# First and last pair of a spectral mixer kernel: other orders of the channel transforms, and the last token transform in other banks

## The chip, the cores and the metric

The kernel runs on one core of one Trainium2 chip. The metric is the device time of one execution in microseconds (us), as the median of several runs of the same kernel. Less than 0.2% (0.73 us) between two kernels is what such a comparison can hardly tell from no change.

## The reference, cut to what matters

The input `x` is 2048 tokens by 512 channels. It is normalised over the channels; then two branches are computed from the same normalised `xn`, multiplied, and added to `x`:

```
xn = layernorm(x)
s  = irfft2(rfft2(xn) * (w_r + 1j * w_i))        # over tokens and channels
g  = silu((gelu(xn.T @ w1 + b1) @ w2 + b2).T)    # a two-layer MLP over the tokens, width 1792
out = x + s * g
```

So a row of the output needs its piece of the inverse spectral transform (`s`) and its piece of the second MLP product (`g`).

## The kernel before, in words

The first 200 us of the program (layer norm, forward transforms, the first MLP product, the spectral filter) are not touched. What is touched is the last stage, the loop over `p` in 0..7. Tokens are held as 16 output tiles of 128 tokens by 512 channels; pair `p` makes tiles `p` and `p + 8` (the names `j0` and `j1`).

**MLP part of a pair.** The second MLP product of a pair is done with a seven-product scheme (as in Strassen's): `ORDER = (1, 2, 5, 6, 3, 7, 4)`. Each product `n` is a group of 21 matmuls of 128x128 weights by 256 columns. The weight tiles are called `w2f`; the moving operands are the forms `fd` (n = 1), `fa` (2, 3), `fc` (5, 6) and `fb` (7, 4), so a reader of the trace can tell the groups by these names. The sums go into the lower halves of three PSUM banks: `bx` (bank 3 for even pairs, bank 2 for odd ones), `by` (bank 4) and `bz` (bank 5). ACT copies some of them out (`p1`, `p5`, `v2`), DVE adds (`c11`, `c12`, `c22`, in the trace all `c`), and ACT makes the gates `g` from the sums with a SiLU. For `n = 4` the gate is taken straight from `bx`.

**Spectral part of a pair.** Three PE blocks make it:

- E, `even_channels`: 16 calls on 64x64 quarters of the array, 32 matmul records (`ps<-cd,yt 64*64 64x64`), into columns 0..255 of banks 6 and 7.
- O, `odd_channels`: 4 calls on the whole array, 8 records (`ps<-cd,yt 128*128 128x128`), into columns 256..511 of banks 6 and 7.
- S, `spectral`: the token transform, 4 calls on 64x64 quarters with 512 columns, 8 records (`ps<-y,cft 64*64 64x512`), into banks 0 and 1.

E and O of a pair need `yt`, which `gathered` collects from `ey` in four steps (letters "g" in the plan: two ACT copies, then two DVE copies). After E and O, `unfolded` (letters "s") copies bank 7 out on ACT (`y<-ps`), makes `es` with five DVE instructions, and then `y` with two more. S of the pair reads `y`. `finish` multiplies a bank of S with a gate into a row tile `r` (two DVE multiplies for a tile) and POOL adds the row to the output in DRAM with two accumulating stores. The last pair's rows are handled without accumulation: `rows` gets the product, `xr` (the input) is added, and SP and ACT store it.

**Order.** Every instruction of this stage is kept in program order on its engine, so the text of the loop is the order of each queue. `SLOTS` says after which of the seven products the spectral block stands (`slot`), and after which products the "g" and "s" steps are done; `PARTS` gives the order of the blocks for each pair, where S is always the one of the pair before. In the first pair, E stands alone one product earlier (`slot - 1`) and O in the slot. In the pairs 2 to 6 the block is E, S, O and stands between the two `fb` products; in pairs 1 and 7 it is S, E, O, and in pair 7 it stands after the second `fc` product. After the block, `finish` is called for both tiles of the pair before. In the last pair, S of the pair itself stands after product 7 (`k == 5`), followed by `finish` for its own tiles, the left half of tile 15 at the very end.

Lines: `SLOTS` 38-40, `PARTS` 44, `gathered` 953, `even_channels` 966, `odd_channels` 977, `unfolded` 984, `spectral` 1006, `finish` 1022, the loop 1038-1100.

Of the kernel before, what the change touches and what calls it, by code (L numbers as in the profile page):

```python
# [36 lines left out]

SLOTS = ((6, {3: "gggg", 6: "s"}), (5, {0: "s", 1: "sgg", 2: "gg", 5: "s", 6: "s"}),
         (5, {0: "s", 1: "gg", 2: "gg", 5: "s", 6: "s"}),
         (3, {0: "s", 1: "gg", 2: "gg", 3: "s", 4: "ss"}))  # L40

PARTS = ("O", "SEO", *["ESO"] * 5, "SEO")

KD = np.concatenate([np.arange(0, 256, 4), np.arange(2, 256, 4), np.arange(1, 256, 2)])

# [94 lines left out]
def spectral_mixer_kernel(tc, x, w1, b1, w2, b2, wk, we, wx, c_f, c_ft, c_d, c_i, c_g, c_h, out):  # L142
    nc = tc.nc
    V, A, G, T, SY = nc.vector, nc.scalar, nc.gpsimd, nc.tensor, nc.sync
# [5 lines left out]
    def mirrored(t, turned):  # L150
        v = t.rearrange("p (h q c) -> p h q c", q=2, c=P)
        return v[:, :, 0], v[:, :, 1, ::-1] if turned else v[:, :, 1]
# [9 lines left out]
    with tc.tile_pool(name="ps", bufs=1, space=PSUM) as psp, ExitStack() as left, ExitStack() as right:  # L162
        ps = psp.tile([P, 8, 512], F32, name="ps")
        pers = pool(left, "left", "pers", 1)
        cf = pers.tile([P, 64], F32, name="cf")
        cft = pers.tile([P, P + 2], F32, name="cft")
# [294 lines left out]
        T = Kept(T, keep)  # L461
# [46 lines left out]
        for j in range(NJ):  # L508
            more = j + 1 < NJ
# [24 lines left out]
            start, more_stats = j < 3, j + 3 < NJ  # L534
# [38 lines left out]
            if more:  # L573
# [3 lines left out]
                if FIRST <= j < FIRST + NE:  # L577
                    i = j - FIRST
# [206 lines left out]
        for n in range(8):  # L785
            a, b, c, d, e, f = PACE[n]
# [12 lines left out]
        NP, HD = NJ // 2, D // 2  # L799
# [38 lines left out]
        def sums_of_blocks():  # L838
            added_up("a12", "s1")
            added_up("a11", "a12")  # L840
# [58 lines left out]
        left_, right_, whole = slice(0, HD), slice(HD, D), slice(0, D)  # L899
        quarter_rows = slice(0, P), slice(P, HD)  # L900

        def banks(p):
            return ps[:, 3 - p % 2, :HD], ps[:, 4, :HD], ps[:, 5, :HD]
# [33 lines left out]
        V, A, SY, G = (Kept(e, keep) for e in (nc.vector, nc.scalar, nc.sync, nc.gpsimd))  # L937
# [3 lines left out]
        def new_sums(p):  # L941
            return (fp.tile([P, 2, 2, 2, P], F32, name=f"es{p}", tag="es"),
                    fp.tile([P, 2, 2, 2, P], F32, name=f"y{p}", tag="y"))

        def new_gates(p):
            return [fp.tile([P, D], F32, name=f"g{j}", tag="g", bufs=4) for j in (p, p + NP)]


        first_sums, gates = new_sums(0), {0: new_gates(0)}
# [3 lines left out]
        def gathered(p):  # L953


            yt = fp.tile([P, 2, 4, 2, 64], F32, name=f"yt{p}", tag="yt")
            yts[p] = yt
            for i, j in enumerate((p, p + NP)):
                for h in range(2):
                    to = yt[:, i, :, h ^ i].rearrange("p b (s c) -> p b s c", c=2)  # L960
                    yield V.tensor_copy(to, ey[:, :, h::2, j]) if i else A.activation(to, ey[:, :, h::2, j], AF.Copy)

        def tokens_of(yt, i, b):
            return yt[:, i, b].rearrange("p e c -> p (e c)")

        def even_channels(p):


            for i in range(2):
                for s in range(2):  # L970
                    at = slice(128 * i + 64 * s, 128 * i + 64 * s + 64)
                    for e in range(2):
                        for r, rows in enumerate((slice(0, 64), slice(64, P))):
                            T.matmul(ps[64 * e:64 * e + 64, 6 + r, at], yts[p][rows, i, 2 * s, e], ci[rows, 2 * s, :64],
                                     start=True, stop=True)

        def odd_channels(p):

            for i in range(2):
                for s in (1, 0):  # L980
                    at = 256 + 128 * s
                    T.matmul(ps[:, 6 + i, at:at + P], tokens_of(yts[p], i, 2 * s + 1), ci[:, 2 * s + 1], start=True, stop=True)

        def unfolded(p):
# [18 lines left out]
            ys[p] = y.rearrange("p i h q c -> p i (h q c)")  # L1003
            yield

        def spectral(p):

            y = ys.pop(p)
            for e, cols in enumerate((slice(0, 64), slice(64, P))):
                for r, rows in enumerate((slice(0, 64), slice(64, P))):  # L1010
                    i = e ^ r
                    T.matmul(ps[cols, i], cft[rows, cols], y[rows, i], start=True, stop=True)

        def gate(g, j, cols, src, scale):
            A.activation(g[:, cols], src, AF.Silu, bias=b2t[:, j:j + 1], scale=scale)

        def summed(name, a, b):
            t = fp.tile([P, HD], F32, name=name, tag="c", bufs=2)
            V.tensor_add(t, a, b)
            return t  # L1020

        def finish(g, j, cols):
            r = last_rows[:, j // NP] if last_rows is not None else fp.tile([P, D], F32, name=f"r{j}", tag="r", bufs=2)
            for to, a, b in zip(mirrored(r[:, cols], True), mirrored(ps[:, j // NP, cols], False), mirrored(g[:, cols], False)):
                V.tensor_mul(to, a, b)
            if last_rows is not None:
                for part in quarter_rows if cols is left_ else (cols,):
                    V.tensor_add(r[:, part], r[:, part], xr[j // NP][:, part])
            for queue, (rows, tokens) in zip((SY, SY if cols is right_ else A), halved):
                if last_rows is None:  # L1030
                    G.dma_start(out[tokens, j, cols], r[rows, cols], accum_op=ALU.add)
                else:
                    queue.dma_start(out[tokens, j, cols], r[rows, cols])

        yts, ys, pieces = {}, {}, iter(())
        last_rows = None

        for p in range(NP):
            j0, j1 = p, p + NP
            more = p + 1 < NP  # L1040
            if p:
                gates[p] = new_gates(p)
            g0, g1 = gates[p]
            bx, by, bz = banks(p)
            slot, plan = SLOTS[min(p, 2) + (not more)]
            gathering = gathered(p)
            for k, n in enumerate(ORDER):
                started = not p and k < 2
                if not started:
                    products(p, n)  # L1050
                if n == 1 and p:
                    p1 = copied(f"p1_{p}", bx, w2p)
                elif n == 5:
                    p5 = copied(f"p5_{p}", bz, fp)
                elif n == 6:
                    v2 = copied(f"v2_{p}", bx, fp)
                elif n == 7:
                    c22 = summed(f"c22_{p}", bx, p5)
                if n == 3 and more:
                    c12 = summed(f"c12_{p}", bz, v2)  # L1060
                if not started:
                    ready.extend(w for w in [next(wforms, None)] if w is not None)
                if n == 2:
                    c11 = summed(f"c11_{p}", by, p1)
                elif n == 6:
                    gate(g0, j0, left_, c11, 1.0)
                elif n == 3 and more:
                    gate(g0, j0, right_, c12, 1.0)
                elif n == 7:
                    gate(g1, j1, right_, c22, -1.0)  # L1070
                elif n == 4:
                    for cols in (left_,) if more else quarter_rows:
                        gate(g1, j1, cols, bx[:, cols], -1.0)
                if not p and k == slot - 1:
                    even_channels(p)
                if k == slot:
                    for part in PARTS[p]:
                        {"S": spectral, "E": even_channels, "O": odd_channels}[part](p - (part == "S"))
                    yts.pop(p)
                    pieces = unfolded(p)  # L1080
                    if p:
                        for g, j in zip(gates.pop(p - 1), (j0 - 1, j1 - 1)):
                            finish(g, j, whole)
                for what in plan.get(k, ""):
                    next(gathering if what == "g" else pieces)
                if n == 3 and not more:
                    gate(g0, j0, right_, summed(f"c12_{p}", bz, v2), 1.0)
                if more and n == 7:
                    sums_of_blocks()
                if not more and k == 2:  # L1090
                    xr = [where.tile([P, NH * P], F32, name=f"xr{i}", tag="s1", bufs=1)[:, :D] for i, where in enumerate((w2p, fp))]
                    for to, j in zip(xr, (j0, j1)):
                        for rows, tokens in halved:
                            SY.dma_start(to[rows], x[tokens, j])
                if not more and k == 5:
                    spectral(p)
                    last_rows = fp.tile([P, 2, D], F32, name="rows", tag="yt")
                    finish(g0, j0, whole)
                    finish(g1, j1, right_)
# [38 lines left out]
```

## Time and profile before

| | |
|---|---|
| median of 3 runs | 364.88 us (364.87 to 364.95) |
| the profiled execution: its own time | 365.01 us |
| its span on the core | 363.2 us |
| mean granted TensorE clock | 0.996 |
| PE busy | 357.3 us, 98% of the span |
| DVE busy | 307.4 us, 85% |
| ACT busy | 210.8 us, 58% |
| POOL busy | 87.2 us, 24% |

The span is the time from the first to the last instruction on the core; the profiled execution's own time is 1.8 us longer. In the rows of the trace, times count from the start of the span. A row of the timeline has the start, the length, the engine, the line (in this stage always 139, the helper that records an instruction), the operation, output and input tiles by name, the shape and the count; in square brackets stands how long the engine had been idle, and what ended the wait. Matmul ends are modelled: the start of one group to the start of the next is the safer measure of a group. PEld is the weight load that goes with a matmul.

### The profile page before, as it was taken

How to read it: one execution, taken by the hardware profiler on the slowest of the kernel's cores; microseconds unless marked ns; L12 is line 12 of the kernel's file. 1: busy time of each engine (PE TensorE's matmuls, PEld its weight loads, DVE VectorE, ACT ScalarE, POOL GpSimd, SP SyncE). 2: the span in 40 equal slices, each digit the busy share in tenths (PEclk: the TensorE clock that was granted, in tenths of full speed). 3: DMA queues.
4: the chain of work that ended last, by engine and by line, in shares of the span. 5: the costliest groups of instructions: out<-in, count | busy, mean ns of one | idle time of the engine just before them, and what ended most of it. 6: DMA issues, size and time to landing. Idle time of an engine off the chain costs nothing.

```text
span 363.2 us, 8851 instructions
## 1 busy us (share of the span) xinstructions
PE 357.3 (98%) x3476; PEld 310.4 (85%) x3476; DVE 307.4 (85%) x590; ACT 210.8 (58%) x385; POOL 87.2 (24%) x134
## 2 busy tenths in 40 slices
PE   8999999999999999999999999999999999999994
PEld 7788888888777788777888999999898989898993
DVE  5899999967799996999995988687887878787974
ACT  4877778867534425756337884646464546565431
POOL 4233333323222022220120001050504132230330
PEclk9999999999999999999999999999999999999998
DMA  7978999306695686996568288698888989898624
GB/s 211 253 181 205 219 289 317 143 0 158 174 264 188 192 249 178 253 239 208 175 213 181 101 227 174 180 188 203 195 192 203 188 216 175 233 151 219 113 27 90
DMA packets 33293, 68.66 MB, mean 189 GB/s; under 512 B 4612, under 2 KB 19380, under 8 KB 33124
## 3 DMA queue, kind: packets, MB, share of 16 engines
q1 hardware_dynamic: 24276, 42.44, 41.2%
q0 software_dynamic: 8496, 25.01, 32.1%
q10 hardware_dynamic: 480, 0.66, 0.6%
q8 instruction: 27, 0.44, 0.5%
q14 instruction: 14, 0.11, 0.1%
HBM read 59.70 MB, written 8.13 MB: 187 GB/s over the span
## 4 chain that ended last, share of the span: by engine, by line
PE 97%; DMA 1%; DVE 1%; ACT 0%; issue 0%; DVEq 0%
PE ps L139 97%; DMA x<-in_x_dram 1%; DVE rows L139 0%; DVE stm L244 0%; DVE h L272 0%; ACT g L139 0%; DVE tm L229 0%; ACT sdm L223 0%; DVEq L1134 0%; DVE mvm L220 0%; DVE rsm L230 0%; DVE r0m L228 0%; DVE v2m L221 0%; DVE v2m L222 0%; DVEq L469 0%
## 5 line engine op out<-in xcount | busy, mean ns | idle before, releaser
L139 PE MATMUL ps<-h,w1h 128*128 128x512 f32 x400 | 116.3, 397 | 0.3 <-DVE h L272 0.3
L139 PEld LDWEIGHTS ps<-h,w1h 128*128 128x128 f32 x400 | 72.9, 188 | 20.1 <-issue 4.9
L139 PE MATMUL ps<-h,w1l 128*128 128x512 f32 x200 | 67.6, 390 | 0.0
L139 DVE TENSOR_TENSOR w2f<-a,w2f 128x896 fp32r<-128x896 f32 x36 | 39.2, 1090 | 16.4 <-ACT w2f L139 16.4
L139 ACT ACTIVATE w2f<-a 128x896 fp32r<-128x896 f32 x36 | 37.1, 1030 | 19.8 <-ACT g L139 8.4
L139 PEld LDWEIGHTS ps<-h,w1l 128*128 128x128 f32 x200 | 37.5, 188 | 8.1
L139 PE MATMUL ps<-fb,w2f 128*128 128x256 f32 x336 | 41.9, 279 | 0.0
L139 POOL DMA_DIRECT2D s<-in_w_dram x14 | 18.3, 1311 | 96.5 <-DVE w2f L139 46.5
L139 PE MATMUL ps<-fa,w2f 128*128 128x256 f32 x336 | 41.2, 277 | 0.0
L139 PEld LDWEIGHTS ps<-fb,w2f 128*128 128x128 f32 x336 | 39.7, 188 | 0.9 <-DVE c L139 0.8
L139 PE MATMUL ps<-fc,w2f 128*128 128x256 f32 x336 | 39.8, 277 | 0.0
L139 PEld LDWEIGHTS ps<-fa,w2f 128*128 128x128 f32 x336 | 39.7, 188 | 0.0
L139 PEld LDWEIGHTS ps<-fc,w2f 128*128 128x128 f32 x336 | 39.0, 188 | 0.0
L155 ACT ACTIVATE w1h<-w1s 128x512 fp32r<-128x512 f32 x26 | 16.2, 631 | 25.1 <-DMA w1s<-in_w_dram 12.0
L139 POOL DMA_DIRECT2D out_dram<-r x28 | 23.6, 1276 | 26.7 <-DVE r L139 26.7
L667 POOL DMA_DIRECT2D xc<-xc x16 | 9.8, 620 | 70.3 <-ACT xc L665 55.1
L308 POOL TENSOR_TENSOR ey<-t 128x256 f32<-128x256 f32 x16 | 15.7, 980 | 44.0 <-DVE t L306 44.0
L139 ACT ACTIVATE w2f<-s 128x896 fp32r<-128x896 f32 x15 | 15.3, 1020 | 14.1 <-PE ps L139 12.3
L139 DVE TENSOR_TENSOR w2f<-s,w2f 128x896 fp32r<-128x896 f32 x15 | 16.3, 1089 | 6.2 <-ACT w2f L139 6.1
L469 DVE TENSOR_TENSOR w1l<-w1r,w1h 128x384 fp32r<-128x384 f32 x32 | 21.3, 670 | 0.0
L268 ACT ACTIVATE h<-x,nbm,rsm 128x256 f32<-128x256 f32 (+1 forms) x34 | 18.4, 591 | 4.2 <-DVE nbm L263 3.2
L139 PE MATMUL ps<-fd,w2f 128*128 128x256 f32 x168 | 20.6, 277 | 0.0
(132 smaller groups left out, 602.1 us busy)
## 6 DMA issues: line engine op xcount, KB each, us to landing
a<-in_w_dram SPq DMA_DIRECT2D x22, 448.0 KB, 4.2
wt<-in_wk_dram POOLq DMA_DIRECT2D x16, 512.0 KB, 6.1
s<-in_w_dram SPq DMA_DIRECT2D x16, 448.0 KB, 4.5
s<-in_w_dram POOLq DMA_DIRECT2D x16, 448.0 KB, 6.7
w1s<-in_w_dram SPq DMA_DIRECT2D x52, 128.0 KB, 5.0
w1r<-in_w_dram SPq DMA_DIRECT2D x28, 192.0 KB, 4.6
xc<-xc POOLq DMA_DIRECT2D x16, 256.0 KB, 3.1
out_dram<-in_x_dram SPq DMA_DIRECT2D x4, 960.0 KB, 6.7
```

What stands on the lines that cost most here:

```text
L139: return lambda *args, **kw: self.keep(operation(*args, **kw))
L155: return A.activation(hi, src, AF.Copy), V.tensor_sub(lo, src, hi.bitcast(F32))
L268: keep(A.activation(to, v, AF.Identity, bias=m["nb"][:, i], scale=m["rs"][:, i, 1:2]))
L308: G.tensor_add(ey[:, 0::3, :, j], a, b)
L469: keep(V.tensor_sub(dst, src, hi.bitcast(F32)))
L667: keep(G.dma_start(*(v.rearrange("p s t c -> p s (t c)") for v in (there[c::2], here[1 - c::2, ::-1]))))
```

## The change

Four things are changed, all in the last stage:

1. First pair: O (instead of E) stands in `slot - 1`, and E (instead of O) in the slot.
2. Last pair: the block is E, S, O instead of S, E, O; the "g" steps are done one product earlier, after products 1 and 2 instead of 2 and 5.
3. Last pair: S no longer writes banks 0 and 1. Tile 7 goes to bank 3, the left half of tile 15 to the upper half of bank 4, and its right half to the upper half of bank 5. The calls that make tile 15 are therefore split into two of 256 columns, so S has six calls instead of four. `finish` reads from these places.
4. Last pair: of the two `finish` calls for the pair before, only the one for tile 6 stays behind the block. The one for tile 14 (two DVE multiplies, two stores on POOL) moves to after product 3, behind the two DVE instructions that make `y` and ahead of the sum `c12`.

```
-         (3, {0: "s", 1: "gg", 2: "gg", 3: "s", 4: "ss"}))
+         (3, {0: "sgg", 1: "gg", 3: "s", 4: "ss"}))
-PARTS = ("O", "SEO", *["ESO"] * 5, "SEO")
+PARTS = ("E", "SEO", *["ESO"] * 6)
...
+        def spectral_places(p):
+            if p < NP - 1:
+                return [[(whole, ps[:, i])] for i in range(2)]
+            return [(whole, ps[:, 3])], [(left_, ps[:, 4, HD:]), (right_, ps[:, 5, HD:])]
+
         def spectral(p):
-            y = ys.pop(p)
+            y, places = ys.pop(p), spectral_places(p)
             for e, cols in enumerate((slice(0, 64), slice(64, P))):
                 for r, rows in enumerate((slice(0, 64), slice(64, P))):
                     i = e ^ r
-                    T.matmul(ps[cols, i], cft[rows, cols], y[rows, i], start=True, stop=True)
+                    for part, to in places[i]:
+                        T.matmul(to[cols], cft[rows, cols], y[rows, i, part], start=True, stop=True)
...
         def finish(g, j, cols):
             r = last_rows[:, j // NP] if last_rows is not None else fp.tile([P, D], F32, name=f"r{j}", tag="r", bufs=2)
-            for to, a, b in zip(mirrored(r[:, cols], True), mirrored(ps[:, j // NP, cols], False), mirrored(g[:, cols], False)):
-                V.tensor_mul(to, a, b)
+            for part, src in spectral_places(j % NP)[j // NP]:
+                if part in (whole, cols):
+                    src = src[:, cols] if part is whole else src
+                    for to, a, b in zip(mirrored(r[:, cols], True), mirrored(src, False), mirrored(g[:, cols], False)):
+                        V.tensor_mul(to, a, b)
...
                 if not p and k == slot - 1:
-                    even_channels(p)
+                    odd_channels(p)
...
-                        for g, j in zip(gates.pop(p - 1), (j0 - 1, j1 - 1)):
+                        for g, j in list(zip(gates[p - 1], (j0 - 1, j1 - 1)))[:1 + more]:
                             finish(g, j, whole)
...
                 if n == 3 and not more:
+                    finish(gates[p - 1][1], j1 - 1, whole)
                     gate(g0, j0, right_, summed(f"c12_{p}", bz, v2), 1.0)
```

## The prediction

> **What bounds the kernel now.** I read the page's shares first, then the chain of waits, then the timeline of PE around the first and the last pair, and last the DVE, ACT and POOL rows of the last pair.
>
> ```profile
> PE   357.3 (98%) x3476; PEld 310.4 (85%) x3476; DVE 307.4 (85%) x590; ACT 210.8 (58%) x385; POOL 87.2 (24%) x134
> ...
> PEclk9999999999999999999999999999999999999998
> ...
> PE 97%; DMA 1%; DVE 1%; ACT 0%; issue 0%; DVEq 0%
> ```
> ```profile
> 6.93 351.73 PE ps L139 x3448
> ```
>
> The chain that ends last runs through PE without a break from 6.93 to 358.67 us. So a part of the change counts only where it makes PE's stream shorter or longer, lets PE wait, or changes what comes after 358.67. The rest is cover. These are PE's rows where the first pair goes over into the second, an E, S, O block of pair 6, and the last pair:
>
> ```profile
> 217.59 0.69 PE L139 MATMUL ps<-cd,yt 64*64 64x64 f32 x32
> 218.22 2.74 PE L139 MATMUL ps<-fb,w2f 128*128 128x256 f32 x21
> 220.80 1.05 PE L139 MATMUL ps<-cd,yt 128*128 128x128 f32 x8
> 221.61 2.72 PE L139 MATMUL ps<-fd,w2f 128*128 128x256 f32 x21
> 224.16 2.63 PE L139 MATMUL ps<-fa,w2f 128*128 128x256 f32 x21
> 226.64 5.11 PE L139 MATMUL ps<-fc,w2f 128*128 128x256 f32 x42
> ...
> 236.62 1.09 PE L139 MATMUL ps<-y,cft 64*64 64x512 f32 x8
> ...
> 332.82 0.69 PE L139 MATMUL ps<-cd,yt 64*64 64x64 f32 x32
> ...
> 335.22 2.63 PE L139 MATMUL ps<-fb,w2f 128*128 128x256 f32 x21
> 337.69 2.54 PE L139 MATMUL ps<-fd,w2f 128*128 128x256 f32 x21
> 340.07 2.54 PE L139 MATMUL ps<-fa,w2f 128*128 128x256 f32 x21
> 342.45 4.92 PE L139 MATMUL ps<-fc,w2f 128*128 128x256 f32 x42
> 347.30 1.09 PE L139 MATMUL ps<-y,cft 64*64 64x512 f32 x8
> ...
> 349.70 2.72 PE L139 MATMUL ps<-fa,w2f 128*128 128x256 f32 x21
> 352.26 2.63 PE L139 MATMUL ps<-fb,w2f 128*128 128x256 f32 x21
> 354.89 1.09 PE L139 MATMUL ps<-y,cft 64*64 64x512 f32 x8
> 355.91 2.74 PE L139 MATMUL ps<-fb,w2f 128*128 128x256 f32 x21
> ```
>
> Two things are to be seen. First, only the S of the last pair (354.89) has a visible wait, treated below. Second, the same group of 21 matmuls has two paces: 2.48 us from start to start at 224.16 to 226.64, and 2.38 us at 337.69 to 340.07. The slow pace holds before the S, E, O block at 236.62, the quick one from there on, and after the S, E, O block at 347.30 the groups are slow again (349.70 to 352.26 is 2.56 us, where the first group after pair 6's block took 335.22 to 337.69, 2.47 us). The granted clock of the page is full on both sides, so it isn't that. The five E, S, O blocks between them change nothing. The rows don't show why.
>
> **First pair: O before E.** E takes 218.22 - 217.59 = 0.63 us of PE, O 221.61 - 220.80 = 0.81 us, and both are still issued, each alone between two groups. The sum is the same: 0. Either block covers the sum `c22` that the next product waits for; O is longer than E, so the cover grows. Only the pace could move: 7 groups (from 218.22 to the block at 236.62) times 0.10 us is 0.7 us, if O ahead of an `fb` group already brings the quick pace, and 0 if not. The nearest rows are E alone at 217.59 and O alone at 220.80; both leave the groups slow. I take 0.
>
> **Last pair: E, S, O and the earlier gather.** An E, S, O block takes 335.22 - 332.82 = 2.40 us, the S, E, O block 349.70 - 347.30 = 2.40 us: 0. E now comes first and needs `yt` by 347.30:
>
> ```profile
> 342.70 1.05 ACT L139 ACTIVATE w2f<-a 128x896 fp32r<-128x896 f32 x1 [1.12 <-PE ps L139]
> 343.64 0.78 ACT L139 ACTIVATE yt<-ey 128x256 f32<-128x256 f32 x2
> ...
> 349.98 0.39 ACT L139 ACTIVATE y<-ps 128x257 f32<-128x257 f32 x1 [0.85 <-PE ps L139]
> ```
> ```profile
> 346.34 1.09 DVE L139 TENSOR_TENSOR w2f<-s,w2f 128x896 fp32r<-128x896 f32 x1 [0.94 <-ACT w2f L139]
> 347.35 0.53 DVE L139 COPY yt<-ey 128x256 f32<-128x256 f32 x2
> ```
>
> The two ACT copies (0.78 us) move into the 1.12 us in which ACT waits for PE ahead of 342.70; the two DVE copies (0.53 us) into the 0.94 us ahead of 346.34. Both are covered, and `yt` is there near 346. Without the cover they would delay a `w2f` that PE needs only later. Cost 0. What the order can bring is the pace: if E, S, O keeps it, as in five blocks out of five, the three groups after the block are 0.1 us shorter each.
>
> **Tile 14 behind `y`.** These are DVE's rows, and PE's weight loads:
>
> ```profile
> 349.77 1.41 DVE L139 TENSOR_TENSOR r<-ps,g 128x256 f32<-128x256 f32 x4
> 351.10 0.61 DVE L139 TENSOR_TENSOR es<-ps,y 128x256 f32<-128x256 f32 x2
> ...
> 353.45 1.29 DVE L139 TENSOR_TENSOR y<-es 128x512 f32<-128x512 f32 x2
> 354.66 0.42 DVE L139 TENSOR_TENSOR c<-ps,v 128x256 f32<-128x256 f32 x1
> 354.99 0.41 DVE L139 TENSOR_TENSOR c<-ps,p 128x256 f32<-128x256 f32 x1
> 356.11 0.76 DVE L139 TENSOR_TENSOR rows<-ps,g 128x256 f32<-128x256 f32 x2 [0.70 <-ACT g L139]
> ```
> ```profile
> 354.86 0.24 PEld L139 LDWEIGHTS ps<-y,cft 64*64 64x64 f32 x8 [0.17 <-issue]
> 355.91 2.54 PEld L139 LDWEIGHTS ps<-fb,w2f 128*128 128x128 f32 x21 [0.81 <-DVE c L139]
> ```
>
> The four multiplies take 351.10 - 349.77 = 1.33 us, so two take 0.67. With two of them gone `es` can start at 350.43; the ACT copy `y` that it needs ends at 350.37. So `y` ends at 354.74 - 0.67 = 354.07. Now the S at 354.89 waits for `y`: it starts 0.15 us after `y` ends. Freed of that it could start behind product 7: at the slow pace 0.07 us earlier (21 matmuls at the slow pace and the usual 0.09 us ahead of a block: 352.26 + 2.47 + 0.09 = 354.82), with the quick pace 0.18 us more (0.09 off the first group after the block, 0.10 off the second), near 354.64. The two multiplies come back between `y` and `c12`, so `c12` stays where it is, 354.66 to 355.08.
>
> **S in six calls, in other banks.** Here a new wait can stand. By the loops the calls come in the order tile 7, tile 15 left, tile 15 right (first 64 output partitions), then tile 15 left, tile 15 right, tile 7 (the other 64). The third call is the first to write bank 5, and `c12` reads the lower half of that bank until 355.08. Behind a waiting third call stand, in PE's queue, two more calls for tile 15 and the second one for tile 7, so more than half of S waits, and the last `fb` group behind it. The trace has no place where PE writes one half of a bank while DVE reads the other, so the cost is bounded from both sides: no wait, S starts at 354.64 and the next `fb` at 354.64 + (355.91 - 354.89) = 355.66, 0.25 us earlier; or a wait as for `y`, 0.15 us after the end of `c12`, so 355.23, and `fb` at 355.23 + 1.02 = 356.25, 0.34 us later. The nearest row is the `fb` group at 355.91, which is put down to a DVE sum `c` that reads the bank it writes, though there the same columns. I take the wait: +0.34 us. The Trainium skill's page PSUM — Partial Sum Buffer (section PSUM bank collisions raise a hardware error) says to guard a bank by bank and quadrant of partitions, not by address, since two engines collide in it even at disjoint columns. By that rule the wait must be there and the sum is +0.34; by addresses alone it would be -0.25. No run here shows a collision.
>
> The split itself: S has 8 records of 599 ns mean and 1.09 us in all:
>
> ```profile
> L139 PE MATMUL ps<-y,cft 64*64 64x512 f32 x64 | 8.5, 599 | 0.0
> ```
>
> So about four run at a time, one per 64x64 quarter. Each call is two records. Two calls of 256 columns stream what one of 512 did in the same quarter, so I take 0. The upper bound is that quarters stop overlapping, below as a rival. The Trainium skill's page TensorE: Matmul & The Clock Gate (section Part 3: Packing small matmuls — row/col tiling) says that matmuls start and end strictly in program order. Taken by the letter, with two records per call in one quarter, even the old S could run only about two at a time; eight records of 599 ns in 1.09 us speak against that reading here; by it the six calls would cost what rival 3 says, or more.
>
> **Behind S.** Everything after it keeps its length: from the `fb` start at 355.91 to the span's end are 363.2 - 355.91 = 7.29 us, less 0.09 if that last group keeps the quick pace. The multiplies of `rows` move with S; they have 0.64 us before the last gates free DVE's last ones:
>
> ```profile
> 359.09 0.55 DVE L139 TENSOR_TENSOR rows<-ps,g 128x128 f32<-128x128 f32 x2 [0.64 <-ACT g L139]
> ```
> ```profile
> 350.81 3.36 POOL L139 DMA_DIRECT2D out_dram<-r  x4 [11.33 <-DVE r L139]
> 360.07 0.50 ACTq L139 DMA_DIRECT2D out_dram<-rows  x1
> ```
> ```profile
> 354.80:355.90 1.10, 1.10 (x9) 0.24 (x8) 0.61 (x2) 0.79 (x2) 0.00 (x0) 1.00 0.95 145
> 355.90:358.60 2.70, 2.70 (x25) 2.54 (x21) 2.27 (x6) 0.12 (x1) 0.00 (x0) 1.00 0.12 20
> ```
>
> Tile 14's two stores on POOL, now the second half of the row at 350.81, are issued from about 355.1 on. Four such stores, first issued at 350.81, had left the DMA engines by 355.90 (share 0.95 before, 0.12 after), 5.1 us. Two of them from 355.1 are through by 360.2 at the latest, just when the last stores of `rows` are issued. Nothing stands behind them on POOL. Cost 0, and some 0.3 us if they still share the engines then.
>
> **The sum**, against the profiled execution's 365.01 us: 0 (first pair) + 0 (block, gather) + 0.34 (S behind `c12`) - 0.09 (last group at the quick pace; the gains of the two groups before are lost in the wait) = +0.25, 365.26 us. The median of the runs is 0.13 us below the profiled execution: 364.88 + 0.25 = 365.1 us.
>
> **The rivals.**
>
> 1. *No wait in bank 5.* S starts at 354.64, `fb` at 355.66 (`c22` ends at 355.40, in time), and the last group saves 0.09: -0.34, 364.5 us. For it: different columns. Against it: same bank. 20%.
> 2. *The quick pace from the first pair on.* For it: every group that went quick follows an O and is an `fb` group, as the group at 218.22 would now be. Against it: O alone at 220.80 left the `fd` groups slow. -0.7 beside the forecast: 364.4 us; with rival 1 as well, which I give half of it, 363.8. 22% in all.
> 3. *Slower: the halves in one quarter hold up the other quarters.* If the third call is placed only after the first two passes of its quarter have streamed, the next tile's calls come later by two half passes for each of the two split tiles: S runs its two rounds in 1.02 us (354.89 to 355.91), so half a round is 0.25 us, and 4 x 0.25 = 1.0 us. With the wait: 0.25 + 1.0 = +1.25, 366.1 us. It decides as soon as the last call of S starts over 0.4 us after `c12` ends. For it: one queue. Against it: E runs 32 records in 0.69 us, so short calls overlap well. 11%.
> 4. *The change at 236.62 turns round:* if S, E, O flips the pace and the first pair already made it quick, the 40 groups from 239 to 347 are slow: +4, 369 us. Against it: E and O alone flip nothing now. 3%.
>
> The forecast has 44%. Telling 0.73 us (0.2%) from no change is about what a measurement can do here. Below 364.15 lie half of rival 2 (11%) and 3% for a quick pace in other groups: 14%. Above 365.6 lie rivals 3 and 4: 14%. Within: 72%. The range leaves out the joint case of 1 and 2, and rival 4: 364.1 to 366.1 us.
>
> **What would show it.** Right: S of the last pair starts in two steps, the first call near 354.6, the rest just after `c12` ends near 355.1; the `fb` group after it starts near 356.25; `y` ends near 354.1; `r` on DVE is x2 twice; groups after the last block are 2.38 apart; groups between 218 and 236 are still 2.48. Wrong: an `fb` start near 355.7 (no wait), groups of 2.38 from 218 on, or an S over 1.6 us long.

## The result, and the profile after

The changed kernel takes 367.48 us (median of 5 runs, 366.55 to 367.80) against 364.88 us: 2.6 us more, a ratio of 1.0066 (95% interval 1.0054 to 1.0078). The forecast was 365.1 us. The profiled execution took 367.44 us with a span of 365.6 us, which is 2.4 us above the span before; the 2.4 us are taken apart here. (Ratios and their intervals, here and below, are worked out from the runs of both kernels; they are not the quotients of the medians.)

The page of the changed kernel, busy time, granted clock in 40 slices, and the chain that ended last by engine:

```profile
PE 359.0 (98%) x3480; PEld 311.7 (85%) x3480; DVE 307.7 (84%) x590; ACT 211.1 (58%) x385; POOL 87.1 (24%) x134
...
PEclk9999999999999999999999999999999999999999
...
PE 97%; DMA 1%; DVE 1%; issue 0%; ACT 0%; DVEq 0%
```

PE got four records more (the split calls) and is busy for 1.7 us more, still with no break in the chain and at a full clock. That leaves 0.7 us of the 2.4 which are not PE's. The timeline of PE, from the first pair to the groups behind the block at 276.50, and in the last pair (the first row, x15, is the part of a group that lies in the stretch shown):

```profile
215.84 1.93 PE L139 MATMUL ps<-fb,w2f 128*128 128x256 f32 x15
...
226.74 5.11 PE L139 MATMUL ps<-fc,w2f 128*128 128x256 f32 x42
...
236.72 1.09 PE L139 MATMUL ps<-y,cft 64*64 64x512 f32 x8
...
241.68 2.63 PE L139 MATMUL ps<-fd,w2f 128*128 128x256 f32 x21
244.15 2.63 PE L139 MATMUL ps<-fa,w2f 128*128 128x256 f32 x21
...
256.61 0.69 PE L139 MATMUL ps<-cd,yt 64*64 64x64 f32 x32
...
276.50 0.69 PE L139 MATMUL ps<-cd,yt 64*64 64x64 f32 x32
...
278.90 2.63 PE L139 MATMUL ps<-fb,w2f 128*128 128x256 f32 x21
281.37 2.54 PE L139 MATMUL ps<-fd,w2f 128*128 128x256 f32 x21
283.75 2.54 PE L139 MATMUL ps<-fa,w2f 128*128 128x256 f32 x21
```
```profile
351.10 2.63 PE L139 MATMUL ps<-fa,w2f 128*128 128x256 f32 x21
353.57 2.54 PE L139 MATMUL ps<-fb,w2f 128*128 128x256 f32 x21
356.04 1.57 PE L139 MATMUL ps<-y,cft 64*64 64x512 f32 x12
357.54 2.75 PE L139 MATMUL ps<-fb,w2f 128*128 128x256 f32 x21
```

Rows of the kernel before that answer to them and were not shown:

```profile
215.74 1.93 PE L139 MATMUL ps<-fb,w2f 128*128 128x256 f32 x15
...
255.86 0.69 PE L139 MATMUL ps<-cd,yt 64*64 64x64 f32 x32
...
275.10 0.69 PE L139 MATMUL ps<-cd,yt 64*64 64x64 f32 x32
...
277.50 2.63 PE L139 MATMUL ps<-fb,w2f 128*128 128x256 f32 x21
```

- **Ahead of the change: +0.10 us.** The last 15 matmuls of the group before the first block begin at 215.84 against 215.74, and the `fc` group at 226.74 against 226.64 has the same delay. The first pair itself is no longer than before.
- **Pairs 2 and 3 (p = 2 and 3): +1.30 us.** A group takes 2.47 us from start to start at the slow pace and 2.38 us at the quick one. Before, the quick pace came with the S, E, O block at 236.62. After, the groups behind that block are still slow (241.68 to 244.15 is 2.47 us), behind the next block too, and the quick pace comes with the E, S, O block at 276.50 (281.37 to 283.75 is 2.38 us). From 256.61 to 276.50 are 19.89 us; the same pair took 275.10 - 255.86 = 19.24 us before. Two pairs, 0.65 us each. The group at 278.90 is 1.40 us late (277.50 before), 0.10 + 1.30.
- **Last pair, up to the last group: +0.23 us.** The two groups and the S behind the block: 357.54 - 351.10 = 6.44 us, against 355.91 - 349.70 = 6.21 us.
- **The end: +0.77 us.** From 357.54 to the end of the span are 8.06 us, against 7.29 us.

One row each of the view that sums a stretch (its length, PE's busy time, records, granted clock, DMA share, GB/s), between the first and the second block of pairs; the kernel before first, then the kernel after:

```profile
239.02:255.86 16.84, 16.84 (x150) 1.00 0.83 176
```
```profile
239.12:256.61 17.49, 17.49 (x150) 1.00 0.80 171
```

The same 150 records at the same granted clock, with a lower DMA share, take 0.65 us more. So neither a lower clock nor more DMA traffic is the cause.

The rows of DVE and of PE's weight loads around the last S, after:

```profile
354.18 1.29 DVE L139 TENSOR_TENSOR y<-es 128x512 f32<-128x512 f32 x2
...
356.04 0.20 PEld L139 LDWEIGHTS ps<-y,cft 64*64 64x64 f32 x4
...
356.05 0.41 DVE L139 TENSOR_TENSOR c<-ps,v 128x256 f32<-128x256 f32 x1
...
356.52 0.63 PEld L139 LDWEIGHTS ps<-y,cft 64*64 64x64 f32 x8 [0.28 <-DVE c L139]
```

`y` is done at 355.47 and no longer holds up S, which begins at 356.04, right behind the quick groups. Four of its loads go ahead; the other eight wait until 356.52, for the sum `c12` that ends at 356.46. S takes 1.50 us up to the next group instead of 1.02.

And the last stores of POOL and of ACT's queue, after:

```profile
352.20 1.66 POOL L139 DMA_DIRECT2D out_dram<-r  x2 [11.34 <-DVE r L139]
...
356.43 1.66 POOL L139 DMA_DIRECT2D out_dram<-r  x2 [2.56 <-DVE r L139]
...
361.70 0.50 ACTq L139 DMA_DIRECT2D out_dram<-rows  x1
```

The last row of ACT's queue is late by 361.70 - 360.07 = 1.63 us, the sum of the first three parts, but the span is late by 2.4. What ends it is in no view of the page: behind its last store each engine has a drain, an instruction that counts as no work. The trace's records of the two that end last (start and end, us):

```
kernel   POOL's drain         SP's last drain ends   the engines' common end begins
before   352.14 to 360.94     362.48                 362.51
after    356.83 to 364.86     364.11                 364.91
```

POOL's drain lasts over 8 us. Before, it began behind stores issued from 350.81 on and was over 1.5 us ahead of SP's. After, it begins behind the stores moved to 356.43 and ends 0.75 us behind SP's. The chain of waits doesn't show it: it ends with DVE's `rows` in both kernels.

### The profile page after: what moved, and what is told of

It reads as the page before. It is cut to its first block, busy times and chain, and to the rows that moved or that the text cites. A ratio compares the mean times of both kernels' runs of the same rounds, so it can differ in the third digit from the quotient of the medians.

```text
span 365.6 us, 8859 instructions
## 1 busy us (share of the span) xinstructions
PE 359.0 (98%) x3480; PEld 311.7 (85%) x3480; DVE 307.7 (84%) x590; ACT 211.1 (58%) x385; POOL 87.1 (24%) x134
## 4 chain that ended last, share of the span: by engine, by line
PE 97%; DMA 1%; DVE 1%; issue 0%; ACT 0%; DVEq 0%
PE ps L139 97%; DMA x<-in_x_dram 1%; DVE rows L139 0%; DVE stm L244 0%; DVE h L272 0%; ACT g L139 0%; DVE tm L229 0%; ACT sdm L223 0%; DVEq L1144 0%; DVE mvm L220 0%; DVE r0m L228 0%; DVE rsm L230 0%; DVE v2m L221 0%; DVE v2m L222 0%; DVEq L469 0%
```

## The experiments

"Quick" and "slow" are the two paces of the product groups; "the quick pace comes at" a time is the start of the first group of that pace. d1, d2, f2 and f3 issue one or two matmuls twice; the second writes the same numbers again. The kernel before, run beside them, took 365.11 us with e1 to e4, 365.14 us with d1 to d4, and 365.10 us with f1 to f4 (medians of 20 to 31 runs).

**e1: the first pair's swap alone.**

```
-PARTS = ("O", "SEO", *["ESO"] * 5, "SEO")
+PARTS = ("E", "SEO", *["ESO"] * 5, "SEO")
...
-                    even_channels(p)
+                    odd_channels(p)
```

> The kernel before with the first pair's swap alone (O one product earlier, E in the slot); the last pair is the old one. Theory now: the swap is what loses the quick pace of the product groups. The groups from 239 on stay at about 2.47 us for one to three pairs more, 0.65 us each, and it differs from run to run: 365.5 to 366.9 us, the tail as before. Rival: the swap costs nothing, and the last pair's change makes all 2.6 us: 364.9 us.

366.30 us, ratio 1.0032 (1.0020 to 1.0044). PE in e1:

```profile
256.47 0.69 PE L139 MATMUL ps<-cd,yt 64*64 64x64 f32 x32
...
276.36 0.69 PE L139 MATMUL ps<-cd,yt 64*64 64x64 f32 x32
...
278.76 2.63 PE L139 MATMUL ps<-fb,w2f 128*128 128x256 f32 x21
281.22 2.54 PE L139 MATMUL ps<-fd,w2f 128*128 128x256 f32 x21
283.60 1.64 PE L139 MATMUL ps<-fa,w2f 128*128 128x256 f32 x13
```

The pair takes 19.89 us, and the quick pace comes at 278.76, as in the changed kernel: the swap alone costs the two pairs.

**e2: the last pair alone** (the changed kernel with the first pair put back).

```
-PARTS = ("E", "SEO", *["ESO"] * 6)
+PARTS = ("O", "SEO", *["ESO"] * 6)
...
-                    odd_channels(p)
+                    even_channels(p)
```

> The changed kernel with the first pair put back (E one product earlier, O in the slot). Theory: groups are quick from 239 on as in the kernel before, in each run; what is left is +0.23 us at the last S and +0.80 us at the end, where POOL's last drain follows tile 14's late stores: 365.9 us, runs close together. Rival: the pace depends on something else in the program, and the slow groups stay: 366.5 us or more.

366.14 us, ratio 1.0035 (1.0022 to 1.0048); the quick pace comes at 239.10, as before the change. By the medians the two halves make 1.2 + 1.0 = 2.2 of the 2.6 us; by the parts listed above they make 1.30 + 1.00 of the 2.40 us, and the 0.10 us ahead of the change belongs to neither.

**e3: e2 with tile 14 finished next to tile 6 again.**

```
-                        for g, j in list(zip(gates[p - 1], (j0 - 1, j1 - 1)))[:1 + more]:
+                        for g, j in list(zip(gates[p - 1], (j0 - 1, j1 - 1))):
...
-                    finish(gates[p - 1][1], j1 - 1, whole)
```

> The last pair's change alone, but with tile 14 finished together with tile 6 again, ahead of the last sums. Theory: POOL's drain ends early again and costs nothing; y ends 0.67 us later, so S starts near its old time, and its third call still waits for c12: 365.1 us. Rival: the 0.8 us at the end comes from the other banks or the split S: 365.9 us.

365.33 us, ratio 1.0009 (0.9999 to 1.0019): 0.8 us less than e2. The rows of e3's last pair:

```profile
350.87 3.35 POOL L139 DMA_DIRECT2D out_dram<-r  x4 [11.34 <-DVE r L139]
...
354.95 1.33 PE L139 MATMUL ps<-y,cft 64*64 64x512 f32 x12 [0.17 <-DVE y L139]
...
356.21 2.73 PE L139 MATMUL ps<-fb,w2f 128*128 128x256 f32 x21
```

The last group begins at 356.21, within 0.01 us of e2's 356.22 below; only the end is earlier. POOL's drain is back at 352.20 to 360.99, under SP's, which ends at 362.78. So the 0.8 us belong to the moved stores. S waits for `y` again, as before the change.

**e4: e2 with the right half of tile 15 in the upper half of bank 6**, which `c12` doesn't touch.

```
-            return [(whole, ps[:, 3])], [(left_, ps[:, 4, HD:]), (right_, ps[:, 5, HD:])]
+            return [(whole, ps[:, 3])], [(left_, ps[:, 4, HD:]), (right_, ps[:, 6, HD:])]
```

> The last pair's change alone, but the right half of tile 15 goes to the upper half of bank 6 instead of bank 5. Theory: S no longer waits for c12 and is about 1.0 us long, the last product group starts 0.48 us earlier than in the last pair alone, but the end stays where POOL's drain puts it: 365.9 us, as the last pair alone. Rival: the end follows PE, and the wait's 0.48 us comes back: 365.4 us. If S is still 1.5 us long, the split into six calls is what costs.

366.09 us, ratio 1.0030 (1.0020 to 1.0040): no different from e2. PE's last S in e2, then in e4 with POOL's stores:

```profile
354.72 1.58 PE L139 MATMUL ps<-y,cft 64*64 64x512 f32 x12
356.22 2.74 PE L139 MATMUL ps<-fb,w2f 128*128 128x256 f32 x21
```
```profile
354.87 1.10 PE L139 MATMUL ps<-y,cft 64*64 64x512 f32 x12
...
355.26 1.66 POOL L139 DMA_DIRECT2D out_dram<-r  x2 [2.57 <-DVE r L139]
...
355.90 2.65 PE L139 MATMUL ps<-fb,w2f 128*128 128x256 f32 x21
```

S takes 1.03 us where it took 1.50: the wait is gone, and the split into six calls costs nothing. But POOL's drain runs from 355.67 to 363.70, 1.3 us beyond SP's at 362.38, so the shorter S gains nothing. With the moved stores, POOL sets the end; without the wait as much as with it.

**d1: the kernel before, with the last O call of the first pair issued twice.** No block changes its place or order.

```
-                    T.matmul(ps[:, 6 + i, at:at + P], tokens_of(yts[p], i, 2 * s + 1), ci[:, 2 * s + 1], start=True, stop=True)
+                    for _ in range(1 + (p == 0 and i == 1 and s == 0)):
+                        T.matmul(ps[:, 6 + i, at:at + P], tokens_of(yts[p], i, 2 * s + 1), ci[:, 2 * s + 1], start=True, stop=True)
```

> The kernel before, but the last of the four O calls of the first pair is issued twice (the same numbers into the same place). Theory P (the pace is settled anew by the fine timing at each break in PE's stream): 0.22 us more of PE can move the onset of the quick pace away from 239, each later pair 0.65 us: anything from 365.0 to 368. Rival Q (the order of the blocks decides): quick from 239 on as before, 365.1 us.

366.57 us, ratio 1.0034 (1.0022 to 1.0046). PE in d1:

```profile
256.80 0.69 PE L139 MATMUL ps<-cd,yt 64*64 64x64 f32 x32
...
276.69 0.69 PE L139 MATMUL ps<-cd,yt 64*64 64x64 f32 x32
...
281.55 2.54 PE L139 MATMUL ps<-fd,w2f 128*128 128x256 f32 x21
```

The call itself takes 0.22 us; the pair takes 19.89 us, and the quick pace comes at 279 as with the swap: 1.30 + 0.22 us. So the order of E and O isn't needed to lose the pace: one call more, 15 us ahead of the block, does the same.

**d2: e1 with the last O call of the second pair twice.**

```
-                    T.matmul(ps[:, 6 + i, at:at + P], tokens_of(yts[p], i, 2 * s + 1), ci[:, 2 * s + 1], start=True, stop=True)
+                    for _ in range(1 + (p == 1 and i == 1 and s == 0)):
+                        T.matmul(ps[:, 6 + i, at:at + P], tokens_of(yts[p], i, 2 * s + 1), ci[:, 2 * s + 1], start=True, stop=True)
```

> The first pair's swap alone, and the last O call of the second pair issued twice. Theory P: the onset moves from the fourth pair's block (279) to another pair, earlier or later, 365.0 to 367. Rival Q: as the first pair's swap alone plus 0.1 to 0.2 us: 366.4 us, quick from 279 on.

366.65 us, ratio 1.0040 (1.0025 to 1.0055). A miss: the quick pace still comes at 279, not at another block, which is what rival Q said.

**d3: the kernel before with E, S, O in the second pair.**

```
-PARTS = ("O", "SEO", *["ESO"] * 5, "SEO")
+PARTS = ("O", *["ESO"] * 6, "SEO")
```

> The kernel before with the second pair's block as E, S, O like the five after it. Theory P: the same length of block, so whether the quick pace comes at 239 is open; if it stays away, 0.65 us for each pair until it comes. Rival R (S, E, O is what switches the pace): never quick before the last pair, about 3.9 us more, 368.8 us, and the last pair's S, E, O makes it quick.

365.72 us, ratio 1.0007 (0.9995 to 1.0019; the runs of the kernel before it was compared with spread from 364.85 to 366.53 us). PE in d3:

```profile
258.94 2.63 PE L139 MATMUL ps<-fb,w2f 128*128 128x256 f32 x21
261.40 2.54 PE L139 MATMUL ps<-fd,w2f 128*128 128x256 f32 x21
263.78 2.54 PE L139 MATMUL ps<-fa,w2f 128*128 128x256 f32 x21
```

The quick pace comes one pair late, without any S, E, O block in front: E, S, O can bring it too, and rival R falls.

**d4: the kernel before with E and O of the first pair in one block.** E stays behind product 7, and O comes one product earlier, right behind E.

```
-SLOTS = ((6, {3: "gggg", 6: "s"}), (5, {0: "s", 1: "sgg", 2: "gg", 5: "s", 6: "s"}),
+SLOTS = ((5, {3: "gggg", 6: "s"}), (5, {0: "s", 1: "sgg", 2: "gg", 5: "s", 6: "s"}),
...
-PARTS = ("O", "SEO", *["ESO"] * 5, "SEO")
+PARTS = ("EO", "SEO", *["ESO"] * 5, "SEO")
...
-                if not p and k == slot - 1:
-                    even_channels(p)
```

> The kernel before with E and O of the first pair together between products 7 and 4, as E, S, O stands in later pairs; one break in PE's stream fewer. Theory P: open; the break saved is about 0.2 us, and the quick pace can come at 219 already, 0.7 us less (364.0 us), or later than 239. Rival Q': a group fb behind O is what makes it quick, so quick from 219 on for certain: 364.0 us.

365.05 us, ratio 0.9995 (0.9986 to 1.0005). The groups of the first pair stay slow, so an `fb` group behind O isn't quick for that alone; the quick pace comes at 239.04, as before.

**f1: the swap, and E, S, O in the second pair.** Diff: as e1, and `PARTS = ("E", *["ESO"] * 6, "SEO")`.

> The first pair's swap, and the second pair's block as E, S, O; nothing else. The slow groups beat: one spacing of 119 ns comes back every nine matmuls, and its place, counted from the last matmul ahead of a block, has gone with the outcome so far: S, E, O made quick from places 1, 4, 7 and left slow from 2, 8; E, S, O made quick from 2, 8 and left slow from 4, 7. Theory P2 (that place, modulo three, together with the kind of block decides): the swap alone stood at place 8 (the changed kernel at 2) ahead of the second pair, so E, S, O there makes it quick at 239: 365.1 us, 1.2 us less than the swap alone. Rival Q2 (the swap itself loses two pairs, and E, S, O in the second pair cost 0.65 us when it was tried alone): 366.3 us or more.

365.25 us, ratio 1.0014 (0.9990 to 1.0039). PE in f1:

```profile
239.29 2.63 PE L139 MATMUL ps<-fb,w2f 128*128 128x256 f32 x21
241.76 2.54 PE L139 MATMUL ps<-fd,w2f 128*128 128x256 f32 x21
244.14 2.54 PE L139 MATMUL ps<-fa,w2f 128*128 128x256 f32 x21
```

With the swap the same E, S, O block that failed at this place in d3 brings the quick pace at once.

**f2 and f3: d4 with E, S, O in the second pair, and the first matmul of the first pair's product 1 issued once more (f2), or twice more (f3).** The diff shows f2's lines; the same kernel with no matmul more was not run.

```
+            for _ in range(1 if not p and n == 1 else 0):
+                T.matmul(o, wf[:, 0, FORMS[0]], form_parts(n, FORMS[0])[0], start=True, stop=True)
```

> E and O of the first pair in one block, the second pair as E, S, O, and the very first matmul of the first product group issued once more (0.12 us; the same numbers, overwritten). Theory P2: one more matmul moves the beat by one place, so the first pair's block meets another residue; if it is the right one, quick from 219 on, 0.7 us less and 0.12 more: 364.5 us; if not, quick from 239 or 259: 365.2 or 365.9 us. Rival (place and residue mean nothing): as without the extra matmul.

> The same with the first matmul issued twice more (0.24 us). Theory P2: the third of the three residues; of the three kernels with none, one and two extra matmuls the onset should differ: 364.6, 365.3 or 366.0 us. Rival: all three alike.

f2: 369.00 us, ratio 1.0101 (1.0079 to 1.0122), more than any number written down. f3: 366.07 us, ratio 1.0020 (1.0010 to 1.0031), the quick pace one pair late. PE in f2:

```profile
257.47 0.69 PE L139 MATMUL ps<-cd,yt 64*64 64x64 f32 x32
...
277.36 0.69 PE L139 MATMUL ps<-cd,yt 64*64 64x64 f32 x32
...
354.36 2.63 PE L139 MATMUL ps<-fa,w2f 128*128 128x256 f32 x21
356.82 2.54 PE L139 MATMUL ps<-fb,w2f 128*128 128x256 f32 x21
```

In f2 all six E, S, O blocks leave the pace slow, 6 x 0.65 = 3.9 us, and the S, E, O block of the last pair, which breaks the quick pace elsewhere, brings it. One matmul of 0.12 us more or less moves the time by 2.9 us (369.00 against 366.07).

**f4: the changed kernel with all three causes mended**: E, S, O in the second pair (f1), tile 14 next to tile 6 (e3), the right half in bank 6 (e4). Diff: those of e3 and e4, and `PARTS = ("E", *["ESO"] * 7)`.

> The changed kernel with three things put right: the second pair's block as E, S, O; tile 14 finished with tile 6 again; the right half of tile 15 in bank 6. Theory: quick from 239, S of the last pair starts behind y near its old time and is 1.0 us long, the end is no longer POOL's: 365.0 us, as before (364.9 with a last group at the quick pace). Rival: one of the three was not a cause: 365.3 (S still waits), 365.9 (the drain) or 366.3 us (the pace).

365.30 us, ratio 1.0028 (1.0000 to 1.0056). That is also the number of the rival in which S still waits, but in the trace the last S starts at 354.96 and the last group at 356.00, 1.04 us later, so the wait in S is gone. The interval is wide because three of the twelve runs took 368.9 to 369.3 us; the other nine took 365.02 to 365.75 us. The profiled execution took 365.11 us, 0.10 us above that of the kernel before. So undoing the three causes takes 2.4 us back by the medians (2.60 above the kernel before, then 0.20), and nothing is won: no kernel here beats the one before.

## Why the prediction was wrong, step by step

**"First pair: O before E ... I take 0."** This step failed: it cost 1.30 us. The prices of the blocks were right (O and E take what they took), and so was the forecast that the groups up to 236 stay slow. Wrong was what the step left out: it asked only whether the swap could bring the quick pace earlier, and took the onset at 236.62 as given. Rival 4 had the sign and the place (the switch at 236.62 turns round), but it asked for a first pair that is already quick, and so had a price of 4 us; the first pair stays slow, and d1 loses the same two pairs with no block in another order. Rival 2, quick from the first pair on, fell with the slow groups at 226.74 and in e1.

What the runs show in its place lies in the single matmuls. In quick groups they start 340 ns per three apart (113.3 ns each), in slow ones 1060 ns per nine (117.8 ns), in a beat in which one spacing of nine is 119 ns. The last spacings (ns) ahead of the block at 236, from the records:

```
before   117 118 118 117 119 117 118 118 118 117 118 118 117 119 117
after    118 118 117 119 117 118 118 117 118 118 118 117 119 117 118
```

Before, the block comes one place behind the 119, after, two places. In the 14 profiles 30 blocks S, E, O or E, S, O follow slow groups. Taken by that place, modulo 3:

```
place mod 3   S, E, O                                     E, S, O
0             quick (f2, last pair)                       slow (f2, six blocks)
1             quick (before, e2, e3, e4, d4)              slow (6 blocks: after, e1, d1, d2 at 256; d3, f3 at 236)
2             slow (after, e1, d1, d2 at 236)             quick (8 blocks: after, e1, d1, d2 at 276; d3, f3 at 256; f1, f4 at 236)
```

There is no exception, and d1, d2 and the swap fall in the same cells. (In d3 at 256 a stray 119 stands two places nearer to the block than the one of the beat; counted is the one of the beat, and by the stray one that block would be an exception.) From quick groups, E, S, O keeps the pace every time, and the S, E, O of the last pair breaks it in all eight kernels that reach it quick. But the table was put together from these traces. Of the runs made to try it, f1 and f4 came out as forecast, and d2 and f2 did not: I couldn't set the place ahead, only read it.

The table holds for blocks of three parts, and the place is not all there is. At the single blocks of the first pair the same place goes with both paces: the kernel before and e4 are the same up to the lone E, e1 and d2 up to the lone O, and in all four the block comes three places behind the 119. The group behind it is slow in the kernel before (218.22) and in e1, and quick in e4 and d2, where it had to wait for a DVE sum (e4, then d2, then e1):

```profile
218.54 2.65 PE L139 MATMUL ps<-fb,w2f 128*128 128x256 f32 x21 [0.16 <-DVE c L139]
```
```profile
218.84 2.65 PE L139 MATMUL ps<-fb,w2f 128*128 128x256 f32 x21 [0.18 <-DVE c L139]
```
```profile
218.26 2.72 PE L139 MATMUL ps<-fb,w2f 128*128 128x256 f32 x21
```

So a wait of under 0.2 us, which some executions have and others of the same instructions don't, goes with the pace as well; that it sets it is not shown. The same rows limit the step's "cover": in these two of the 14 profiles the lone block did not cover the sum.

That the swap moved the place from 1 to 2 and that this goes with the lost pairs is shown. Why such a beat exists, and why a block keeps or breaks it, stays open; nothing in the records shows it.

**"Behind S ... Nothing stands behind them on POOL. Cost 0."** This step failed too: +0.77 us. I asked when the two stores had left the DMA engines (360.2 at the latest) and not when POOL itself is done. Its drain ends some 8.4 us after the last two stores are issued (356.43 to 364.86; in e4 355.26 to 363.70). The trace of before held it: its drain took 8.80 us, and behind stores issued at 355.1 such a drain ends at 363.9 at the earliest, later than SP's end at 362.48. e3 shows it by undoing that one move.

**"S in six calls, in other banks ... I take the wait: +0.34 us."** Right. +0.23 us was measured: the two groups give 0.25 us (353.57 + 2.47 is 356.04, where S begins), S takes 0.48 us more, forecast as 0.59 (it restarts 0.06 us after `c12` ends, not 0.15). e4 shows both parts, the wait and the free split; rivals 1 and 3 fall, though rival 1's -0.25 is what bank 6 gives PE (355.90 - 349.93 = 5.97 us from block to last group, against 6.21 before). The Trainium skill's page PSUM — Partial Sum Buffer (section PSUM bank collisions raise a hardware error) says to guard a bank, not an address; the kernel's wait goes that way, and its price here is the 0.48 us.

**"Last pair: E, S, O and the earlier gather": 0.** Right: the block takes 2.40 us (348.70 to 351.10) as before. `y` is 0.67 us earlier against the rest (354.18 with 1.40 us of delay, 353.45 before), as the step said.

**"- 0.09 (last group at the quick pace)".** Wrong by its size: it measured 0. Behind the lone S the last group is slow again: 357.54 to PE's end at 360.30 is 2.76 us, and 355.91 to 358.67 was 2.76 us before. It is slow in twelve of the 14 profiles and quick in e4 (2.65 us in the row at 355.90, above) and d2, so the gain exists but can't be counted on.

So: forecast 0.34 - 0.09 = +0.25 us; measured +0.23 for the groups and S, +1.30 for the pace, +0.77 for POOL's drain, +0.10 ahead of the change.

## What to carry to other kernels

Where the same group of matmuls shows two paces in one trace at the same clock, the switch between them is a risk in the sum of every edit upstream of it (one call of 0.22 us set it off in d1, d4's moved block didn't), and its price is the difference times all groups behind it (here 0.65 us a pair, up to 3.9 us). Look for the drains behind each engine's last store before moving a store towards the end: the views that count work don't show them, and here a store of POOL had to be issued over 8 us before the end to be free. A gain on PE in the last microseconds (0.24 us in e4) is worth nothing until the engine that ends last is known.

## What the runs showed of the hardware that was not expected

- Two stable paces of the same matmuls at a granted clock of 1.00, 113.3 and 117.8 ns, that hold for tens of microseconds and change, in these 14 traces, only at blocks of another tile shape.
- A sensitivity that the medians hide: in f1 two of twelve runs, and in f4 three, took 368.9 to 369.4 us, 3.6 to 4.1 us above the others, which is what six slow pairs cost in f2; e2, e3 and e4 had one or two such runs each, 1.2 to 1.5 us above their medians. The five runs of the changed kernel spread over 1.25 us, those of the kernel before beside it over 0.08 us, though with f1 to f4 the kernel before spread from 364.93 to 367.47 us. That the onset differs from run to run would explain these; no profile of such a run was taken, so this is not shown.
- POOL's drain takes 8.0 us behind two late stores and 8.8 us behind four earlier ones.
